# Moving the first batch's tail mixing into block 0, with the ScalarE table loaded first and some copies moved to ScalarE

## The chip, the cores and the metric

The kernel runs on one core of a Trainium2 chip. The core has five engines with queues of their own: PE (TensorE, matrix products; its weight loads are listed as PEld), DVE (VectorE), ACT (ScalarE), POOL (GpSimd) and SP (SyncE, which here issues the transfers). They work on SBUF; PE writes its results into PSUM, of which this kernel uses eight banks. The metric is the device time of one execution in microseconds (us); less is better.

## The reference

Two steps follow each other for a batch of 8, with 8 heads, 576 tokens and a head dimension of 64:

```python
kv = np.einsum('bhsd,bhse->bhde', k, v)            # linear attention, no softmax
out = np.einsum('bhsd,bhde->bhse', q, kv)
rms = np.sqrt(np.mean(out * out, axis=-1, keepdims=True) + 1e-06)
x = (out / rms * g_norm)                            # heads side by side: (8, 576, 512)
h = x.transpose(0, 2, 1) @ U @ V                    # mixes tokens, rank 32
u = x + h.transpose(0, 2, 1)
ch = np.maximum(u @ w_ch1, 0.0) @ w_ch2             # 512 -> 2048 -> 512
return u + ch
```

U, V, w_ch1 and w_ch2 arrive as float64 and are decoded to float32 on the chip from their bit patterns.

## The kernel before, in words

**Tiling.** Heads are handled in pairs (128 columns), so a batch has four pairs. The 8 x 576 = 4608 tokens are cut into nine blocks of 512 columns for the feed-forward part, so a block does not end with its batch: block 0 is the first 512 tokens of batch 0, and the last 64 tokens of batch 0 are the first columns of block 1. In a block, f runs over 16 tiles of the 2048 hidden features: `ffn1` (L365) multiplies with w1, `relu` (L372) takes the positive part, `ffn2` (L381) multiplies with w2 into four PSUM banks. Every product is made of three in a shorter format (high x high, high x low, low x high), so activations and weights are kept as a high and a low part. `relu` writes the high part on ScalarE (L377), the low part on VectorE (L378).

**Startup.** Batch 0 has no earlier block to hide behind. Its steps stand in a list `tasks` (L475 to L486), each with a place number from `PLAN` (L39); the list is sorted by that number and written out before block 0. For a pair p the steps are: `kv_step` (k transposed times v, copied into `kvb`), `out_step` (q times kv, five products, and their squares on ScalarE), `stats_step` (sums on VectorE, square root on ScalarE, reciprocal and a refinement on VectorE), `mul_step`, `xsplit_step` (high part `xh` on ScalarE, low part `xl` on VectorE), `turn_step` (transposes x by products with the identity, four 128-token tiles into one bank, `main`), `t_step` (the product with U), `t4_step` (its high and low parts into a tile `t4`), `keep_warm`, `mix_first` and `mix_rest`.

`mix_first` (L334) adds the product of `t4` and V to `main` and writes the high and low part of 512 columns of block 0's input (names `uth`, `utl`). `mix_rest` (L347) does the same for the last 64 tokens: one product with the identity (L350, listed as two instructions), one of `t4` and V (L352), a scaled copy to `ut32` (L353, by the helper at L104). `split_cols(0, p, 1)` then makes from it the high and low part of the first 64 columns of block 1 (L94 and L95). In the startup `mix_rest` stands at `PLAN["mt"]`, after all four `mix_first`; the splits of all four pairs stand in block 0.

`keep_warm` (L329) issues products whose result nobody reads, into a bank called `spare` (name `h`); its stationary operand is the pair's `t4`.

**Block 0 and later.** `prep_schedule(j + 1)` (L495) returns what is to be done beside block j, by half step: entry 2f comes after `relu` of f, entry 2f + 1 after `ffn2` of f - 1. It holds batch 1's steps during block 0. Block 0 also decodes the weights: `decode_w` for the f up to three ahead (L533 to L536). A decode is five instructions on raw bits (absolute value at L81 on ScalarE or at L83 on VectorE, then L84, L85, L87 and L89 on VectorE) and a split (L94 on ScalarE, L95 on VectorE); the first tile of each matrix is decoded in the startup, with temporaries called `early`, all others with the three buffers called `st`. The `t4` tiles of pairs 1 to 3 of batch 0 are taken from the same three buffers (L424).

**Who does what.** `ENG` (L40) names an engine for each use of the helpers `move` (L97), `minus` and `decode`: a is ScalarE, v VectorE, g GpSimd, one letter per pair or use. The helpers' own lines (L102, L104, L108, L110, L114) appear in the profile.

**Order.** The order in the program is a priority. When it is built, a scheduler that plans with estimated durations takes, for each engine, the first instruction in that order that is ready and whose tile has a free buffer; the order that it finds is fixed for each engine's queue. A tile's buffer comes free with the last instruction in the whole program that uses it.

Of the kernel before, what the change touches and what calls it, by code (L numbers as in the profile page):

```python
# [10 lines left out]
F32 = mybir.dt.float32  # L11
# [9 lines left out]
P = 128  # L21
NPAIR = H // 2
NT = 5
MAIN = 4 * P
TAIL = S - MAIN
NF = DF // P
ND = DM // P
# [9 lines left out]
STEPS0 = dict(kv=1, out=2, t=6, mix=11, gap=3)  # L37
AHEAD = dict(w1=3, w2=3)
PLAN = dict(pair=(0, 7, 13, 13), kv=(0, 0, 0, 0), out=(2, 0, 0, 6), stats=(2, 3, 3, 6), mul=(2, 3, 3, 6), xs=(11, 11, 10, 10), tr=(11, 11, 11, 14), t=(14, 14, 12, 14), t4=(18, 18, 14, 18), mix=(18, 23, 21, 23), mt=(42, 42, 42, 42), uv=6, v4=11, w0=49, w1=45, w2=38, w3=49, x0=49, warm=12, fill0=4, fill1=3, fill2=1, fill3=2, u2=60)  # L39
ENG = dict(kv='aaaaa', xh='aaaaa', xl='vvvvv', t4='avva', te='aaaa', uh='vaaa', v4='aggg', wh='ava', wl='vvv', ab='vav', u='agva')  # L40
LOADS = ['uv', 'q1', 'w10', 'kv1', 'w11', 'kv2', 'g', 'q2', 'q3', 'kv3', 'w12', 'w20', 'w13', 'w22', 'w23', 'w21', 'kv4', 'q4']
NBLK = B * S // BLK
ABS_LO = float(np.array([897 << 20], np.uint32).view(np.float32)[0])
# [4 lines left out]
def build(ctx: ExitStack, tc: tile.TileContext, kv_in, kvt0_in, kvt_in, q_in, uv_in, g_in, w1, w2, out):  # L48
    nc = tc.nc

    const = ctx.enter_context(tc.tile_pool(name="const", bufs=1))
# [11 lines left out]
    ut32 = [const.tile([P, S], F32, name=f"ut32_{c}") for c in range(ND)]  # L63
    ident = const.tile([P, P], F32, name="ident")
    g_sb = const.tile([P, 1], F32, name="g_sb")
    eps = const.tile([P, 2], F32, name="eps")
    u2 = const.tile([P, NT, 2 * R], F32R, name="u2")
    v4 = const.tile([P, S], F32R, name="v4")
    kvb = [const.tile([P, P], F32, name=f"kvb{i}") for i in range(2)]

    def weight_slot(name, shape, dtype, which, f):

        return const.tile(shape, dtype, name=name, tag=f"{which}_{f}")

    def decode(raw, tmp, n=None):
# [3 lines left out]
        bits = tmp.bitcast(U32)  # L79
        if n is None or ENG["ab"][n] == "a":  # L80
            nc.scalar.activation(out=tmp, in_=high.bitcast(F32), func=AF.Abs)  # L81
# [10 lines left out]
    def split(hi, lo, src, lo_eng):  # L92

        nc.scalar.copy(out=hi, in_=src)  # L94
        lo_eng.tensor_tensor(out=lo, in0=src, in1=hi.bitcast(F32), op=ALU.subtract)  # L95

    def move(which, n, out, in_, mul=None):  # L97

        e = ENG[which][n]
        if e == "a":  # L100
            if mul is None:
                nc.scalar.copy(out=out, in_=in_)  # L102
            else:
                nc.scalar.mul(out=out, in_=in_, mul=mul)  # L104
        else:
            eng = nc.vector if e == "v" else nc.gpsimd
            if mul is None:
                eng.tensor_copy(out=out, in_=in_)  # L108
            else:
                eng.tensor_scalar(out=out, in0=in_, scalar1=mul, scalar2=None, op0=ALU.mult)  # L110

    def minus(which, n, out, in0, in1):
        eng = nc.vector if ENG[which][n] == "v" else nc.gpsimd
        eng.tensor_tensor(out=out, in0=in0, in1=in1, op=ALU.subtract)  # L114
# [22 lines left out]
    def load_q(b, p):  # L137
        if b == 0 and 0 < p:
            qt = weight_slot(f"q0_{p}", [P, S], F32, "w1", NF - 1 - p)
        else:  # L140
            qt = ldp.tile([P, S], F32, name="q_sb")
        nc.sync.dma_start(out=qt, in_=q_in[b, p])
        loads["q", b, p] = qt
# [23 lines left out]
    def ut_of(j):  # L167
        if j not in ut:
            ut[j] = [utp.tile([P, ND, BLK], F32R, name=f"ut{s}") for s in "hl"]
        return ut[j]  # L170
# [4 lines left out]
    def bank():  # L175
        bank_no[0] += 1
        if startup[0] and bank_no[0] % (7 - NEARLY) >= 3 - NEARLY:
            return ps_y.tile([P, 512], F32, name="y")
        return ps_p.tile([P, 512], F32, name="pp")
# [28 lines left out]
    state = {}  # L208
# [103 lines left out]
    def split_cols(b, c, part, lo_eng):  # L312

        m = BLK * (b + 1) - S * b
        uh, ul = ut_of(b + part)
        if part == 0:
            src, lo = ut32[c][:, 0:m], BLK - m
        else:
            src, lo = ut32[c][:, m:S], 0
        n = src.shape[-1]  # L320
        hi, lo = uh[:, c, lo:lo + n], ul[:, c, lo:lo + n]
        if b == 0:
            split(hi, lo, src, lo_eng)
        else:
            nc.scalar.mul(out=hi, in_=src, mul=g_sb)  # L325
            nc.vector.scalar_tensor_tensor(out=lo, in0=src, scalar=g_sb, in1=hi.bitcast(F32),  # L326
                                           op0=ALU.mult, op1=ALU.subtract)

    def keep_warm(p, n):  # L329

        for _ in range(n):
            nc.tensor.matmul(spare, lhsT=state[0, p]["t4"], rhs=v4[:, 0:MAIN], start=True, stop=True)

    def mix_first(p):  # L334

        s = state[0, p]
        main = s["main"]
        for a in (0, 2):
            own = main.rearrange("p (i a j) -> p i a j", a=4, j=32)[:, :, a:a + 2]
            v = v4[:, QO[a]:QO[a] + 2 * QL[a]].rearrange("p (a t) -> p a t", a=2)[:, :, 0:P]  # L340
            nc.tensor.matmul(own, lhsT=s["t4"], rhs=v.rearrange("p a (i j) -> p i a j", j=32), start=False, stop=(a == 2))
        uh, ul = ut_of(0)
        move("uh", p, uh[:, p], main, g_sb)
        nc.vector.scalar_tensor_tensor(out=ul[:, p], in0=main, scalar=g_sb, in1=uh[:, p].bitcast(F32),
                                       op0=ALU.mult, op1=ALU.subtract)

    def mix_rest(p):  # L347
        s = state[0, p]
        tail = bank()[:, 0:TAIL]
        nc.tensor.matmul(tail, lhsT=s["x"][0:TAIL, 4, :], rhs=ident[0:TAIL, 0:TAIL], start=True, stop=False)  # L350
        v = v4[:, 0:2 * QL[0]].rearrange("p (a t) -> p a t", a=2)[:, :, P:]
        nc.tensor.matmul(tail.rearrange("p (a j) -> p a j", a=2), lhsT=s["t4"], rhs=v, start=False, stop=True)  # L352
        move("te", p, ut32[p][:, MAIN:S], tail, g_sb)  # L353
# [54 lines left out]

    load_kv(0, 0)
    load_q(0, 0)  # L410
    nc.vector.memset(kvb[0], 0.0)
    spare = ps_h.tile([P, BLK], F32, name="h")
    for _ in range(PLAN["warm"]):
        nc.tensor.matmul(spare[:, 0:P], lhsT=kvb[0], rhs=kvb[0], start=True, stop=True)
    nc.scalar.sqrt(out=kvb[0][:, 0:1], in_=kvb[0][:, 0:1])
    x0 = [x_sb] + [weight_slot(f"x{p}", [P, NT, P], F32, "w2", NF - 4 - p) for p in range(1, NPAIR)]
    xhl0 = [weight_slot(f"x{n}0", [P, nt, P], F32R, "w1", f) for n, nt, f in (("h", NT, NF - 1), ("l", 4, NF - 6))]
    for t in x0:
        nc.gpsimd.memset(t[TAIL:P, 4, :], 0.0)
    nc.gpsimd.memset(kvb[1], 0.0)  # L420
    nc.gpsimd.memset(eps[:, 0:1], 1e-6)
    nc.gpsimd.memset(eps[:, 1:2], -0.5e-6)
    make_identity(nc, ident)
    t40 = {p: st.tile([P, P], F32R, name="st") for p in (1, 2, 3)}  # L424
    early = [weight_slot(f"early{i}", [P, DM], F32, f"w{i + 1}", 9) for i in range(2)]
# [49 lines left out]
    tasks = [(PLAN["uv"], uv_step), (PLAN["v4"], v4_step), (PLAN["u2"], u2_step)]  # L475
    for p in range(NPAIR):
        for name, what in (("kv", kv_step), ("out", out_step), ("stats", stats_step), ("mul", mul_step),
                           ("xs", xsplit_step), ("tr", turn_step), ("t", t_step), ("t4", t4_step)):
            tasks.append((PLAN["pair"][p] + PLAN[name][p], lambda what=what, p=p: what(0, p)))
        tasks.append((PLAN["pair"][p] + PLAN["mix"][p], lambda p=p: keep_warm(p, PLAN[f"fill{p}"])))  # L480
        tasks.append((PLAN["pair"][p] + PLAN["mix"][p], lambda p=p: mix_first(p)))
        tasks.append((PLAN["pair"][p] + PLAN["mt"][p], lambda p=p: mix_rest(p)))
    ahead = {"w1": NEARLY, "w2": 1}
    for f in range(NEARLY):
        tasks.append((PLAN[f"w{f}"], lambda f=f: decode_w("w1", f, early[f % 2], min(f, 1))))
# [9 lines left out]
    def prep_schedule(b):  # L495

        todo = {}
        if 0 < b <= B:
            todo[1] = [lambda: [split_cols(b - 1, c, 1, nc.vector) for c in range(ND)]]
        if b < B:  # L500
            for p in range(NPAIR):
                steps = STEPS0 if b == 1 else STEPS
                base = steps["gap"] * p

                def kv(p=p):
                    kv_step(b, p)
                    nxt = (b, p + 1) if p + 1 < NPAIR else (b + 1, 0)
                    if nxt[0] < B:
                        load_kv(*nxt)

                def o(p=p):
                    for what in (out_step, stats_step, mul_step, xsplit_step, turn_step):
                        what(b, p)
                    nxt = (b, p + 1) if p + 1 < NPAIR else (b + 1, 0)
                    if nxt[0] < B:
                        load_q(*nxt)

                def t(p=p):
                    t_step(b, p)
                    t4_step(b, p)  # L520

                for at, what in (("kv", kv), ("out", o), ("t", t), ("mix", lambda p=p: mix_step(b, p))):
                    todo.setdefault(base + steps[at], []).append(what)
        return todo
# [3 lines left out]
    for j in range(NBLK):  # L528
        todo = prep_schedule(j + 1)
# [88 lines left out]
```

## Time and profile before

| | |
|---|---|
| median of 3 runs | 933.15 us (931.9 to 934.48) |
| the profiled execution's own time | 932.47 us |
| its span (first to last instruction) | 930.7 us |
| PE, DVE, ACT, POOL busy | 913.9, 430.4, 265.2, 48.1 us |
| mean granted TensorE clock | 0.994 of full |
| instructions | 12300 |

The profiled execution took 932.47 us, of which the span is 930.7. A line such as L350 is a line of the kernel before. In rows of a group, the first number behind the bar is busy time in us, the next the mean of one in ns, and behind the second bar stands the idle time of the engine just ahead of these instructions, with what ended most of it. Rows in order of time begin with the start in us and the duration. A product on float32 operands appears as two PE instructions. PE instructions overlap, so a difference of starts says more than a duration.

### The profile page before, as it was taken

To read this page: it belongs to the slowest core of one execution; us is meant where nothing else is said; L and a number is where in the kernel's file an instruction comes from. 1 tells how busy PE (TensorE), PEld (TensorE's weight loads), DVE (VectorE), ACT (ScalarE), POOL (GpSimd) and SP (SyncE) were. 2 spreads that over 40 slices of the span, in tenths; PEclk is the share of its full clock that TensorE was granted. 3 is DMA by queue.
4 is the path that set the end of the run, shared out by engine and by line. 5 is a ranking of instruction groups with operands and counts; after the bars stand their busy time and mean duration, and the time that the engine had idled before them with its cause. 6 is when DMAs were issued, how large, how long until landed. Compare 5 with 4: busy or idle time off the path is not lost.

```text
span 930.7 us, 12300 instructions
## 1 busy us (share of the span) xinstructions
PE 913.9 (98%) x4570; PEld 764.7 (82%) x4570; DVE 430.4 (46%) x945; ACT 265.2 (28%) x598; POOL 48.1 (5%) x67
## 2 busy tenths in 40 slices
PE   8899989999999999999999999999999999999998
PEld 8778867888888888888888888888788888888887
DVE  6899997444364345434344445434344331112112
ACT  5455654322232223222222223222222221111110
POOL 3000002000020002000200001000200020002000
PEclk9899999999999999999999999999999999999999
DMA  8952213221122121211121112212110010001001
GB/s 345 407 223 71 63 38 107 69 56 55 49 97 59 31 77 63 84 31 57 64 69 54 40 59 74 82 31 73 58 50 25 13 46 1 1 0 46 1 1 46
DMA packets 45036, 65.49 MB, mean 70 GB/s; under 512 B 9904, under 2 KB 28080, under 8 KB 44976
## 3 DMA queue, kind: packets, MB, share of 16 engines
q1 hardware_dynamic: 44976, 64.71, 21.2%
q8 instruction: 36, 0.59, 0.3%
q14 instruction: 24, 0.20, 0.1%
HBM read 46.97 MB, written 9.44 MB: 61 GB/s over the span
## 4 chain that ended last, share of the span: by engine, by line
PE 89%; DVE 5%; DMA 3%; SPq 1%; issue 0%; ACT 0%; POOL 0%; DVEq 0%; POOLq 0%
PE y L385 39%; PE h L368 13%; PE h L369 13%; PE h L370 13%; PE pp L195 3%; PE pp L218 2%; DMA w2raw<-w 1%; DMA g_sb<-g_in 1%; PE pp L290 1%; SPq L278 1%; PE pp L292 1%; DVE utl L326 1%; PE pp L360 1%; PE pp L220 1%; PE pp L385 1%; DVE hl L378 1%
## 5 line engine op out<-in xcount | busy, mean ns | idle before, releaser
L385 PE MATMUL y<-hh,w2s 128*128 128x512 f32 x1144 | 374.2, 394 | 2.0 <-ACT hh L377 2.0
L385 PEld LDWEIGHTS y<-hh,w2s 128*128 128x128 f32 x1144 | 207.4, 188 | 42.6 <-ACT hh L377 3.7
L378 DVE SCALAR_TENSOR_TENSOR hl<-h,hh 128x512 fp32r<-128x512 f32 x142 | 97.9, 690 | 295.7 <-ACT hh L377 294.6
L368 PE MATMUL h<-uth,w1s 128*128 128x512 f32 x568 | 224.2, 395 | 1.8 <-DVE hl L378 1.8
L385 PE MATMUL y<-hl,w2s 128*128 128x512 f32 (+1 forms) x572 | 221.2, 387 | 1.9 <-DVE hl L378 1.9
L369 PE MATMUL h<-utl,w1s 128*128 128x512 f32 x568 | 222.1, 391 | 0.0
L370 PE MATMUL h<-uth,w1s 128*128 128x512 f32 x568 | 221.6, 390 | 0.0
L377 ACT ACTIVATE hh<-h 128x512 fp32r<-128x512 f32 x142 | 84.9, 598 | 387.1 <-PE h L370 387.0
L368 PEld LDWEIGHTS h<-uth,w1s 128*128 128x128 f32 x568 | 106.7, 188 | 27.0 <-DVE hl L378 3.9
L385 PEld LDWEIGHTS y<-hl,w2s 128*128 128x128 f32 x572 | 107.4, 188 | 24.1 <-DVE hl L378 2.0
L370 PEld LDWEIGHTS h<-uth,w1s 128*128 128x128 f32 x568 | 106.7, 188 | 23.2 <-DVE w1s L95 0.3
L369 PEld LDWEIGHTS h<-utl,w1s 128*128 128x128 f32 x568 | 106.9, 188 | 21.1
L397 POOL TENSOR_TENSOR st<-st,utl 128x512 f32<-128x512 f32 x32 | 40.7, 1294 | 773.1 <-DVE st L396 770.0
L362 DVE TENSOR_TENSOR ut<-pp,ut 128x288 f32<-128x288 f32 x56 | 25.0, 456 | 51.3 <-DMA ut<-xt 40.8
L396 DVE TENSOR_TENSOR st<-y,uth 128x512 f32<-128x512 f32 x32 | 21.3, 687 | 44.5 <-PE y L385 32.7
L325 ACT ACTIVATE uth<-ut,g_sb 128x448 fp32r<-128x448 f32 (+7 forms) x56 | 27.7, 532 | 46.5 <-DVE ut L362 39.5
L234 DVE TENSOR_REDUCE sums<-x 128x10 f32<-128x640 f32 x32 | 26.2, 818 | 22.6 <-ACT x L222 22.6
L326 DVE SCALAR_TENSOR_TENSOR utl<-ut,g_sb,uth 128x448 fp32r<-128x448 f32 (+7 forms) x56 | 26.9, 513 | 11.8 <-ACT uth L325 8.0
L195 PE MATMUL pp<-kv_sb 128*128 128x128 f32 x232 | 32.3, 280 | 0.0
L195 PEld LDWEIGHTS pp<-kv_sb 128*128 128x128 f32 x232 | 30.4, 197 | 0.9
L218 PE MATMUL pp<-kvb,q_sb 128*128 128x128 f32 x224 | 30.3, 280 | 0.0
L102 ACT CAST xh<-x 128x640 fp32r<-128x640 f32 x32 | 23.2, 726 | 24.8 <-DVE x L249 24.8
(188 smaller groups left out, 682.9 us busy)
## 6 DMA issues: line engine op xcount, KB each, us to landing
kv_sb<-kv_in SPq DMA_DIRECT2D x29, 512.0 KB, 3.6
q_sb<-q_in SPq DMA_DIRECT2D x29, 288.0 KB, 2.8
w1raw<-w SPq DMA_DIRECT2D x16, 512.0 KB, 9.9
w2raw<-w SPq DMA_DIRECT2D x16, 512.0 KB, 10.1
out<-st SPq DMA_DIRECT2D x32, 256.0 KB, 2.0
ut<-xt SPq DMA_DIRECT2D x224, 20.0 KB, 1.8
ut<-xt SPq DMA_DIRECT2D x224, 16.0 KB, 1.8
kvt_sb<-kvt_in SPq DMA_DIRECT2D x27, 128.0 KB, 3.2
```

Of the source, the lines that this page charges most:

```text
L195: nc.tensor.matmul(pp[:, 0:P], lhsT=m[:, i * P:(i + 1) * P], rhs=m[:, MAIN + i * P:MAIN + (i + 1) * P], start=(i == 0 and b < NATIVE), sto ...
L218: nc.tensor.matmul(big[:, i * P:(i + 1) * P], lhsT=qt[:, TAIL + i * P:TAIL + (i + 1) * P], rhs=kb, start=True, stop=True)
L234: nc.vector.tensor_reduce(out=sums.rearrange("p (i h) -> p i h", h=2), in_=xv, axis=AX.X, op=ALU.add)
L325: nc.scalar.mul(out=hi, in_=src, mul=g_sb)
L326: nc.vector.scalar_tensor_tensor(out=lo, in0=src, scalar=g_sb, in1=hi.bitcast(F32), op0=ALU.mult, op1=ALU.subtract)
L368: nc.tensor.matmul(h, lhsT=w1s[f][0][:, d, :], rhs=uh[:, d, :], start=(d == 0), stop=False)
L369: nc.tensor.matmul(h, lhsT=w1s[f][0][:, d, :], rhs=ul[:, d, :], start=False, stop=False)
L370: nc.tensor.matmul(h, lhsT=w1s[f][1][:, d, :], rhs=uh[:, d, :], start=False, stop=(d == ND - 1))
L377: nc.scalar.activation(out=hh, in_=h, func=AF.Relu)
L378: nc.vector.scalar_tensor_tensor(out=hl, in0=h, scalar=0.0, in1=hh.bitcast(F32), op0=ALU.max, op1=ALU.subtract)
L385: nc.tensor.matmul(acc, lhsT=w2s[f][w][:, c, :], rhs=h[:, cols], start=(f == 0 and w == 0 and h is hh), stop=(f == NF - 1 and w == 1))
L397: nc.gpsimd.tensor_tensor(out=o, in0=o, in1=ul[:, c, :].bitcast(F32), op=ALU.add)
```

## The change

- `mix_rest` leaves the startup's list. In block 0's list its pair p stands at half step 1 + 2p, followed by that pair's `split_cols` (before, the four splits stood together at half step 1). Later batches keep their splits as they were.
- The products of `keep_warm` take their stationary operand from `v4` (V's parts) and not from the pair's `t4`.
- The constants `eps` get a third column; VectorE sets them first of all, and a square root on them is ScalarE's first instruction. The square root on `kvb` after the warm-up products is gone.
- `ENG`: the copies of `t4` for pairs 1 and 2, the high part of pair 0's mixed columns, and the first step of the decode for the two weight tiles of the startup are ScalarE's instead of VectorE's.

```diff
-ENG = dict(..., t4='avva', te='aaaa', uh='vaaa', ..., ab='vav', ...)
+ENG = dict(..., t4='aaaa', te='aaaa', uh='aaaa', ..., ab='aaa', ...)
...
-    eps = const.tile([P, 2], F32, name="eps")
+    eps = const.tile([P, 3], F32, name="eps")
...
-            nc.tensor.matmul(spare, lhsT=state[0, p]["t4"], rhs=v4[:, 0:MAIN], start=True, stop=True)
+            nc.tensor.matmul(spare, lhsT=v4[:, 0:P], rhs=v4[:, 0:MAIN], start=True, stop=True)
...
     load_q(0, 0)
+    nc.vector.memset(eps[:, 0:1], 1e-6)
+    nc.vector.memset(eps[:, 1:2], -0.5e-6)
+    nc.scalar.sqrt(out=eps[:, 2:3], in_=eps[:, 0:1])
     nc.vector.memset(kvb[0], 0.0)
...
-    nc.scalar.sqrt(out=kvb[0][:, 0:1], in_=kvb[0][:, 0:1])
...
-    nc.gpsimd.memset(eps[:, 0:1], 1e-6)
-    nc.gpsimd.memset(eps[:, 1:2], -0.5e-6)
...
-        tasks.append((PLAN["pair"][p] + PLAN["mt"][p], lambda p=p: mix_rest(p)))
...
         if 0 < b <= B:
-            todo[1] = [lambda: [split_cols(b - 1, c, 1, nc.vector) for c in range(ND)]]
+            if b == 1:
+                for p in range(NPAIR):
+                    todo[1 + 2 * p] = [lambda p=p: mix_rest(p), lambda p=p: split_cols(0, p, 1, nc.vector)]
+            else:
+                todo[1] = [lambda: [split_cols(b - 1, c, 1, nc.vector) for c in range(ND)]]
```

More of the change, by code (lines that the diff above doesn't have):

```diff
@@ L39 @@
 PLAN = dict(pair=(0, 7, 13, 13), kv=(0, 0, 0, 0), out=(2, 0, 0, 6), stats=(2, 3, 3, 6), mul=(2, 3, 3, 6), xs=(11, 11, 10, 10), tr=(11, 11, 11, 14), t=(14, 14, 12, 14), t4=(18, 18, 14, 18), mix=(18, 23, 21, 23), mt=(42, 42, 42, 42), uv=6, v4=11, w0=49, w1=45, w2=38, w3=49, x0=49, warm=12, fill0=4, fill1=3, fill2=1, fill3=2, u2=60)
-ENG = dict(kv='aaaaa', xh='aaaaa', xl='vvvvv', t4='avva', te='aaaa', uh='vaaa', v4='aggg', wh='ava', wl='vvv', ab='vav', u='agva')
+ENG = dict(kv='aaaaa', xh='aaaaa', xl='vvvvv', t4='aaaa', te='aaaa', uh='aaaa', v4='aggg', wh='ava', wl='vvv', ab='aaa', u='agva')
 LOADS = ['uv', 'q1', 'w10', 'kv1', 'w11', 'kv2', 'g', 'q2', 'q3', 'kv3', 'w12', 'w20', 'w13', 'w22', 'w23', 'w21', 'kv4', 'q4']
```

## The prediction, made before the changed kernel ran

> **What bounds the kernel now.** I read the page's engine line first, then a table of busy time by stage that I cut at the places where the clock and the chain of waits change, then the chain itself, then the instructions in order of time between 6 and 41 us. The page says that PE is busy throughout:
>
> ```profile
> PE 913.9 (98%) x4570; PEld 764.7 (82%) x4570; DVE 430.4 (46%) x945; ACT 265.2 (28%) x598; POOL 48.1 (5%) x67
> ```
>
> That is an average over stages with different limits, and the change touches only the first of them. Busy time by stage (columns: stretch in us, length, then busy us and instruction count of PE, PEld, DVE, ACT and POOL, the granted clock, the DMA share, GB/s):
>
> ```profile
> 6.50:9.90 3.40, 1.76 (x14) 1.45 (x13) 2.24 (x6) 2.79 (x7) 0.00 (x0) 1.00 1.02 412
> 9.90:13.30 3.40, 3.40 (x17) 3.22 (x16) 2.89 (x6) 2.18 (x9) 2.92 (x7) 0.50 0.79 305
> ...
> 24.00:36.20 12.20, 11.01 (x84) 9.43 (x84) 10.56 (x26) 4.96 (x12) 0.10 (x1) 1.00 1.04 407
> ...
> 37.20:40.60 3.40, 1.11 (x6) 0.90 (x6) 3.34 (x10) 1.78 (x7) 0.00 (x0) 1.00 1.02 407
> 40.60:47.40 6.80, 6.80 (x25) 5.95 (x26) 6.25 (x13) 4.08 (x11) 0.00 (x0) 0.50 1.03 411
> 47.40:107.10 59.70, 58.98 (x293) 48.71 (x293) 58.93 (x128) 34.23 (x71) 0.00 (x0) 1.00 0.36 128
> 107.10:153.20 46.10, 41.21 (x208) 32.67 (x206) 45.37 (x103) 25.17 (x52) 0.00 (x0) 1.00 0.20 58
> 153.20:240.00 86.80, 86.80 (x445) 73.14 (x446) 41.72 (x97) 25.58 (x62) 5.13 (x4) 1.00 0.22 64
> ```
>
> From 47.4 to 153.2 us VectorE is full: 58.93 of 59.70 and 45.37 of 46.10. In the second of these stretches PE idles 46.10 - 41.21 = 4.9 us. The chain of waits says who sets the end of that stretch:
>
> ```profile
> 150.79 0.69 DVE x L247
> 151.70 0.84 DVE xt L275
> 152.55 0.59 DVE hl L378
> 153.18 0.50 PE h L368
> ```
>
> So block 0 ends when VectorE has worked off the weight decodes, the splits and batch 1's preparation. Behind 153 us PE is full (86.80 of 86.80) and VectorE half idle; none of that work is touched, so I let it follow block 0 unchanged. **The question is therefore how much earlier VectorE gets through its queue**, and not how much PE work is saved.
>
> **The change part by part.** First, the table. These are instructions in order of time (start, duration, engine, line, operation):
>
> ```profile
> 7.39 0.49 PE L199 MATMUL pp<-kvt_sb 64*128 64x128 f32 x2
> 7.51 1.28 ACT L415 ACT_TABLE_LOAD   x1
> 8.80 0.20 ACT L415 ACTIVATE kvb<-kvb 128x1 f32<-128x1 f32 x1
> 9.04 0.43 ACT L102 COPY kvb<-pp 64x64 f32<-64x64 f32 x2
> 9.52 1.77 PE L218 MATMUL y<-kvb,q_sb 128*128 128x128 f32 x8 [1.64 <-ACT kvb L102]
> ```
>
> Pair 0's product is finished at 7.39 + 0.49 = 7.88 us, but its copy waits until 9.04 behind a second table load (1.28) and a square root (0.20) whose operand the warm-up matmuls still read. With a square root first, on a constant that VectorE has just set, there is one load, ahead of all data. The absolute values decode later under the square root's table with no further load (the L81 instructions below), so I expect no second one. Pair 0 gains up to 9.04 - 7.88 = 1.16 us. Against it stand two more one-column memsets on VectorE ahead of the one that the warm-up waits for. The trace has no such row; the 128-column memset took 0.17 us, so I bound the two between 0 and 0.34 and count 0.2. As for what arrives at the end of the stage: later pairs wait for loads of their own, so between 0 and 1.16; I take 0.5.
>
> On this load the Trainium skill, page "ScalarE: Activation LUTs", section "What ACT_TABLE_LOAD costs", gives about 1283 ns plus about 1380 ns of drain, 2.66 us for each switch. The trace agrees on the 1.28; the next activation starts 0.01 us behind it, so no such drain shows. By the page pair 0 would gain 2.66; I keep the row.
>
> Second, the moves from VectorE to ScalarE (groups: count, then busy us and mean ns of one):
>
> ```profile
> L110 DVE TENSOR_SCALAR uth<-pp,g_sb 128x512 fp32r<-128x512 f32 x1 | 0.8, 751 | 0.4 <-DMA w2raw<-w 0.4
> ...
> L83 DVE TENSOR_SCALAR early<-w2raw 128x512 uint32<-128x512 uint32 x1 | 0.4, 427 | 0.3 <-POOL early L427 0.3
> L83 DVE TENSOR_SCALAR early<-w1raw 128x512 uint32<-128x512 uint32 x1 | 0.4, 421 | 0.0
> ...
> L108 DVE CAST st<-y 64x128 fp32r<-64x128 f32 x1 | 0.3, 282 | 0.0
> L108 DVE CAST st<-pp 64x128 fp32r<-64x128 f32 x1 | 0.3, 275 | 0.0
> ```
>
> ```profile
> L81 ACT ACTIVATE st<-w1raw 128x512 f32<-128x512 f32 x5 | 3.4, 671 | 0.2 <-DVE w2s L95 0.2
> ...
> L104 ACT ACTIVATE uth<-pp,g_sb 128x512 fp32r<-128x512 f32 x2 | 1.4, 689 | 4.3 <-PE pp L341 2.6 <-PE pp L352 1.6
> ...
> L102 ACT CAST t<-pp 64x128 fp32r<-64x128 f32 x1 | 0.3, 260 | 0.1
> ```
>
> VectorE loses 0.751 + 0.427 + 0.421 + 0.282 + 0.275 = 2.16 us. ScalarE gains 0.689 + 2 x 0.671 + 2 x 0.260 = 2.55 us, and it has room: 4.96 busy of 12.2 us from 24.0 to 36.2. If that cover were gone (ScalarE busy with something else when pair 0's mixing lands), what is late is that pair's low part at L344, by at most one such instruction, 0.7 us. The whole 2.16 lies ahead of 36.2 us, where VectorE still waits for others now and then, so it counts in full only if the next work is ready. Bounds 0 and 2.16. The three on pairs 0 to 2 (1.31 together) stand in VectorE's queue ahead of pair 3's statistics; I take 1.0.
>
> Third, the last 64 tokens. Their four mixings (L350 twice, L352 once, each) leave the startup, and the unread products of `keep_warm` no longer wait for the pair they keep warm. In order of time:
>
> ```profile
> 34.08 0.43 PE L350 MATMUL y<-ident,x 64*128 64x64 f32 x2
> 34.44 0.30 PE L352 MATMUL y<-v,t 128*128 128x64 f32 x1
> ...
> 35.75 0.48 PE L369 MATMUL pp<-utl,w1s 128*128 128x512 f32 x1
> ...
> 36.65 0.40 PE L287 MATMUL y<-xl,u4w 128*64 128x128 f32 x4
> 37.31 0.26 ACT L102 CAST st<-y 64x128 fp32r<-64x128 f32 x1
> ...
> 38.01 0.35 DVE L95 TENSOR_TENSOR utl<-ut,uth 128x64 fp32r<-128x64 f32 x2
> 38.40 0.28 DVE L301 TENSOR_TENSOR st<-y,st 64x128 fp32r<-64x128 f32 x1
> ...
> 38.74 0.73 PE L332 MATMUL h<-v,st 128*128 128x512 f32 x2 [1.69 <-DVE st L301]
> 39.31 0.40 PE L341 MATMUL pp<-v,st 128*128 128x256 f32 x2
> ...
> 40.49 0.71 PE L368 MATMUL pp<-uth,w1s 128*128 128x512 f32 x1 [0.75 <-ACT uth L104]
> ```
>
> Pair 3 is the last to be mixed. Three tails sit in PE's queue between its own products (34.08 to 35.75, 1.67 us, 0.56 each), two of their splits stand ahead of its L301 on VectorE (0.35), and two unread products ahead of its mixing (38.74 to 39.31, 0.57). Taken out, block 0's last quarter of f = 0 could start 1.67 + 0.35 + 0.57 = 2.59 us before 40.49. The same PE work, 4 x 0.56 = 2.2 us, comes back in block 0, now behind f = 0 to 3. It is covered by PE's 4.9 us of idling before 153.2; without that cover it would cost 2.2. The splits (two ScalarE and one VectorE instruction per pair) run behind 36.2 us already, so VectorE's full stretch neither gains nor loses by them.
>
> What VectorE sees of the 2.59 is another matter. Its long queue starts with the decodes into the `st` buffers, and these are three, all held by the t4 of pairs 1 to 3 until the last product that reads them, which is the tail's:
>
> ```profile
> 35.03 0.30 PE L352 MATMUL y<-v,st 128*128 128x64 f32 x1
> ...
> 35.58 0.65 ACT L81 ACTIVATE st<-w1raw 128x512 f32<-128x512 f32 x1
> ...
> 36.26 0.43 DVE L84 TENSOR_SCALAR st<-st 128x512 f32<-128x512 f32 x1 [0.83 <-ACT st L81]
> ```
>
> The first decode starts 0.25 us behind the tail product that frees its buffer. In the changed program the tails stand behind f = 0's work in priority, but they need nothing later than pair 3's t4, so an order made by what is ready can still fill PE's waits with them. Bounds for VectorE: +2.59 (all of the chain's gain arrives) and -3.3 (below, the slower rival). I take 1.5, since pair 3's shorter chain is sure and the buffers' release only possibly late.
>
> **Sum:** 0.5 + 1.0 + 1.5 = 3.0 us. The profiled execution took 932.47 us (span 930.7 and 1.8 around it): 929.5. The median of the runs, 933.15, is 0.7 above that execution; the same step from it ends at 930.2. I say 929.8, between the two. What a measurement can tell from no change is about 0.3%, 2.8 us, so this stands at the edge.
>
> **Rivals.** *Hidden anyway.* VectorE and ScalarE get idle instead of early: loads and PE still pace the startup (PE 11.01 of 12.20 from 24.0 to 36.2, DMA full), the tails are again put into the same gaps and the buffers come free at the same moment. Only the table and a part of the moves count, about 1.0: 931.5. For it speaks that VectorE has slack before 36 us (10.56 of 12.20), against it that pair 3's own chain is what is cut.
>
> *The buffers are late: slower.* If the tails of pairs 1 to 3 really run in the order written, behind the rest of f = 0 and batch 1's first products, the first `st` buffer comes free not at 35.3 but about when the last one did, 39.55 plus its 0.19; the decode of w1's f = 1 then reaches VectorE 4.2 us later than 36.26. Less the 0.83 that it idles there already, 3.3 us are lost, and a full queue doesn't regain them: 935.8. It decides from the point where the buffers come more than about 2 us later than now, since the table and the moves bring 1.5. For it: the priority written; against it: PE idles just then (1.11 busy of 3.40 from 37.2).
>
> *PE sets the end and keeps its clock: more.* PE ran at half clock from 40.6 to 47.4, behind a stretch with 1.11 busy of 3.40; if free fillers and the shorter chain remove that, PE has 6.8 x 0.5 = 3.4 us more. It counts only if VectorE's queue gives way as well, so on top of the forecast at best: 926. The same happened once before, 9.9 to 13.3 at 0.50 behind 1.76 busy of 3.40.
>
> On this the Trainium skill, page "TensorE: Matmul & The Clock Gate", section "What's actually happening", has the half rate follow a window of about 3.4 us that is idle. Both windows here were partly busy, so by its wording neither drop would have come; the rows decide. By the page there would be nothing to win, and the forecast, which counts nothing for the clock, stays as it is.
>
> **How the numbers follow.** Forecast 0.45 (its own range 927.5 to 931), hidden anyway 0.27, late buffers 0.20, PE's clock too 0.08. Measured against the median, faster by over 0.3% means below 930.35: most of the forecast (0.39) and the last case (0.08) give 0.47; the rest of the forecast and nearly all of hidden anyway 0.32; late buffers and a tail of hidden anyway 0.21. The range runs from 925.5, the best case, to 935.8, the slower one.
>
> **What would show it.** Right: one table load, pair 0's L218 near 8.4; no L83, L110 or 64-row L108 on VectorE; the first L84 into `st` before 35 us; d = 3 of f = 0 at 37 to 38; VectorE's last decode and the first chain step on PE alone about 3 us earlier than 153.2, and the stretch behind it as long as before. Wrong: that L84 at 36 or later, a VectorE with more idle time before it and the same end, or tails (L352) behind f = 1 with decodes waiting for buffers.

## The result: 2.2% slower

The changed kernel took 953.73 us in the median of four runs (953.6 to 955.36), the kernel before 933.34 beside it (931.9 to 934.48). The ratio is 1.0222 with a 95% interval of 1.0207 to 1.0237: about 20 us slower, outside the predicted range of 925.5 to 935.8. The profiled execution took 953.6 us, with a span of 951.8 where the one of before had 930.7. Of all executions below, one of e11 took 1847.9 us, in a slow state, and its times are given without that one.

**What the 21.1 us of span are.** The engine line of the changed kernel's page:

```profile
PE 917.5 (96%) x4570; PEld 767.0 (81%) x4570; DVE 430.1 (45%) x942; ACT 267.9 (28%) x602; POOL 48.4 (5%) x65
```

PE has the same 4570 instructions. It is busy for 917.5 us instead of 913.9, which is 3.6 more, and idle for 951.8 - 917.5 = 34.3 us instead of 930.7 - 913.9 = 16.8, which is 17.5 more. Together that is 21.1: PE waits, and a part of its work runs longer.

**Where it waits.** Busy time by stage of the changed kernel (stretch, length, then busy us and instruction count of PE, PEld, DVE, ACT, POOL, granted clock, DMA share, GB/s):

```profile
36.20:47.40 11.20, 5.96 (x26) 4.22 (x26) 7.30 (x17) 5.77 (x14) 0.00 (x0) 0.76 1.03 409
47.40:69.40 22.00, 12.07 (x53) 9.70 (x51) 16.18 (x31) 8.20 (x17) 0.00 (x0) 0.74 0.60 221
69.40:92.00 22.60, 14.95 (x61) 12.21 (x60) 22.10 (x53) 13.92 (x35) 0.22 (x1) 0.62 0.29 89
92.00:165.00 73.00, 72.13 (x361) 59.75 (x360) 72.03 (x157) 41.38 (x83) 0.00 (x0) 1.00 0.17 49
```

The same stretches of the kernel before, from 36.2 us on:

```profile
36.20:47.40 11.20, 8.76 (x42) 7.46 (x41) 10.52 (x24) 6.86 (x20) 0.00 (x0) 0.70 1.02 408
47.40:69.40 22.00, 21.62 (x96) 17.57 (x95) 21.69 (x48) 11.87 (x22) 0.00 (x0) 1.00 0.57 219
69.40:92.00 22.60, 22.29 (x121) 18.88 (x122) 22.14 (x48) 13.04 (x29) 0.00 (x0) 1.00 0.23 73
92.00:165.00 73.00, 68.08 (x345) 54.92 (x344) 67.31 (x150) 38.54 (x83) 5.13 (x4) 1.00 0.23 71
```

From 36.2 to 92 us PE is busy for 5.96 + 12.07 + 14.95 = 32.98 us where it had 8.76 + 21.62 + 22.29 = 52.67: 19.7 us of busy time are missing, and PE ran 140 instructions instead of 259. From 47.4 to 69.4 us VectorE, which was full there, idles too (16.18 of 22.00): no engine sets the pace in this stretch, only waits do. From 69.4 on VectorE is full again (22.10 of 22.60), but PE still waits. From 92 to 165 us PE is busier than before (72.13 against 68.08) and so gets some 4 us back.

**What is waited for: the decodes.** Instructions of the changed kernel in order of time (start, duration, engine, line; idle time before in brackets), between 40 and 61 us:

```profile
40.84 0.43 PE L350 MATMUL pp<-ident,x 64*128 64x64 f32 x2 [1.19 <-DVE hl L378]
41.21 0.30 PE L352 MATMUL pp<-v,st 128*128 128x64 f32 x1
42.23 0.43 DVE L84 TENSOR_SCALAR st<-st 128x512 f32<-128x512 f32 x1 [0.72 <-ACT st L81]
...
56.22 0.66 ACT L81 ACTIVATE st<-w2raw 128x512 f32<-128x512 f32 x1 [0.76 <-DVE w1s L95]
56.91 0.43 DVE L84 TENSOR_SCALAR st<-st 128x512 f32<-128x512 f32 x1 [0.73 <-ACT st L81]
58.32 0.30 PE L352 MATMUL pp<-v,st 128*128 128x64 f32 x1
...
59.34 0.62 ACT L94 CAST w2s<-st 128x512 fp32r<-128x512 f32 x1 [2.46 <-DVE st L89]
59.99 0.69 DVE L95 TENSOR_TENSOR w2s<-st,w2s 128x512 fp32r<-128x512 f32 x1 [0.74 <-ACT w2s L94]
60.72 0.66 ACT L81 ACTIVATE st<-w2raw 128x512 f32<-128x512 f32 x1 [0.76 <-DVE w2s L95]
```

The first decode into an `st` buffer reaches VectorE at 42.23 us, right behind the tail product at 41.21 that frees the buffer; before, it was at 36.26. The other tails that read `st` run as late as 58.32 and 72.2, so until then two of the three buffers, or one, stay held. One decode begins when the last has ended: the absolute values (L81) start at 41.54, 46.32, 51.72, 56.22, 60.72 and 65.21, that is 4.5 to 5.4 us apart. In the round that is shown VectorE waits 0.73 for L81 and 0.74 for L94.

**And a second wait.** Further on in the same order of time:

```profile
71.83 0.43 PE L350 MATMUL pp<-ident,x 64*128 64x64 f32 x2 [2.25 <-DVE ts L305]
72.20 0.30 PE L352 MATMUL pp<-v,st 128*128 128x64 f32 x1
72.39 0.22 POOL L427 MEMSET early<- 128x1 f32 x1 [55.55 <-PE pp L350]
73.69 0.66 ACT L81 ACTIVATE early<-w2raw 128x512 f32<-128x512 f32 x1
...
84.41 0.80 PE L385 MATMUL y<-hh,w2s 128*128 128x512 f32 x1 [1.52 <-ACT w2s L102]
```

The rows of the same memset and the same product in the kernel before:

```profile
33.22 0.10 POOL L427 MEMSET early<- 128x1 f32 x1 [17.07 <-DVE xh L263]
...
49.82 1.07 PE L385 MATMUL y<-hh,w2s 128*128 128x512 f32 x4
```

POOL's one-column memset at L427 claims the second `early` buffer, in which the first tile of w2 is decoded. That buffer lies in the same place in SBUF as pair 3's x. In the kernel before, POOL waited 17.1 us for that place, and its release came from pair 3's L263; here it waits 55.55, for pair 3's tail (L350). So w2's tile 0 is decoded from 73.69, and `ffn2` begins at 84.41 instead of 49.82. `h` has one bank, and `hh` and `hl` have two buffers each, so `ffn1` can't run ahead for long meanwhile.

What the prediction forecast of the startup itself did come, in order of time of the changed kernel (its L414 is L411 of the kernel before):

```profile
0.89 0.17 DVE L414 MEMSET kvb<- 128x128 f32 x1
...
7.71 0.41 ACT L102 COPY kvb<-pp 64x64 f32<-64x64 f32 x2
8.17 1.16 PE L218 MATMUL y<-kvb,q_sb 128*128 128x128 f32 x8 [1.23 <-ACT kvb L102]
...
21.15 2.49 PE L332 MATMUL h<-v 128*128 128x512 f32 x10
23.48 1.05 PE L272 MATMUL pp<-ident,x 128*128 128x128 f32 x8
24.37 1.06 PE L218 MATMUL y<-kvb,q 128*128 128x128 f32 x8
...
38.12 0.48 PE L368 MATMUL pp<-uth,w1s 128*128 128x512 f32 x1
```

Pair 0's copy starts at 7.71 instead of 9.04, and the last quarter of f = 0 at 38.12 instead of 40.49. What is new here is the ten unread products in one piece, 2.49 us from 21.15, ahead of a turn (L272) and a query product (L218, before at 23.60).

### The profile page after: what moved, and what is told of

Its sections match the earlier page's. It is cut to its first block, busy times and chain, and to the rows that moved or that the text cites. A ratio compares the mean times of both kernels' runs of the same rounds, so it can differ in the third digit from the quotient of the medians.

```text
span 951.8 us, 12297 instructions
## 1 busy us (share of the span) xinstructions
PE 917.5 (96%) x4570; PEld 767.0 (81%) x4570; DVE 430.1 (45%) x942; ACT 267.9 (28%) x602; POOL 48.4 (5%) x65
## 4 chain that ended last, share of the span: by engine, by line
PE 85%; DMA 7%; DVE 6%; SPq 1%; issue 0%; POOL 0%; ACT 0%; DVEq 0%; POOLq 0%; ACTq 0%
PE y L385 38%; PE h L368 13%; PE h L369 13%; PE h L370 13%; DMA w2raw<-w 3%; PE pp L195 2%; PE pp L218 2%; DMA q_sb<-q_in 1%; DVE st L87 1%; DMA w1raw<-w 1%; PE pp L290 1%; DMA kv<-kv_in 1%; DVE st L89 1%; PE pp L360 1%; PE pp L292 1%; PE pp L385 1%
## 5 line engine op out<-in xcount | busy, mean ns | idle before, releaser
L378 DVE SCALAR_TENSOR_TENSOR hl<-h,hh 128x512 fp32r<-128x512 f32 x142 | 97.9, 689 | 311.2 <-ACT hh L377 310.1
L218 PE MATMUL pp<-kvb,q_sb 128*128 128x128 f32 x224 | 31.6, 287 | 8.2 <-ACT kvb L102 8.1
L218 PEld LDWEIGHTS pp<-kvb,q_sb 128*128 128x128 f32 x224 | 29.7, 201 | 9.4 <-ACT kvb L102 8.8
## 6 DMA issues: line engine op xcount, KB each, us to landing
w1raw<-w SPq DMA_DIRECT2D x16, 512.0 KB, 10.2
```

Source lines behind the costliest of these rows:

```text
L218: nc.tensor.matmul(big[:, i * P:(i + 1) * P], lhsT=qt[:, TAIL + i * P:TAIL + (i + 1) * P], rhs=kb, start=True, stop=True)
L378: nc.vector.scalar_tensor_tensor(out=hl, in0=h, scalar=0.0, in1=hh.bitcast(F32), op0=ALU.max, op1=ALU.subtract)
```

## The experiments

The theory after the result: the tails run late, and until then they hold two things, the `st` buffers (hold 1) and the place of pair 3's x (hold 2). Rivals: it is another part of the change; one hold alone is enough of a cause; or it is the lateness itself and not what is held.

### Which part of the change

**e1.** The kernel before with only the tails moved:

```diff
-        tasks.append((PLAN["pair"][p] + PLAN["mt"][p], lambda p=p: mix_rest(p)))
...
+            if b == 1:
+                for p in range(NPAIR):
+                    todo[1 + 2 * p] = [lambda p=p: mix_rest(p), lambda p=p: split_cols(0, p, 1, nc.vector)]
```

> The kernel before with nothing but the tails moved into block 0. If the move alone makes the loss (both theories below): 952 to 956 us, with the first product of ffn2 near 84 us again and three late tails. If the loss needs the other three edits as well (free fillers that shift the order, ScalarE's longer queue): within 5 us of 933.

Measured: 955.58 us, ratio 1.0241 (1.0226 to 1.0255). The tails that read `st` run at 40.86, 57.90 and 72.19 us and the first `ffn2` at 85.00, much as in the changed kernel. The move alone makes the whole loss.

**e2.** The changed kernel with the tails back in the startup (table, ScalarE's copies and the unread products on V stay; the expectations call the unread products fillers):

```diff
+        tasks.append((PLAN["pair"][p] + PLAN["mt"][p], lambda p=p: mix_rest(p)))
...
-            if b == 1:
-                for p in range(NPAIR):
-                    todo[1 + 2 * p] = ...
```

> The changed kernel with the tails back in the startup: table first, moves to ScalarE and free fillers alone. By the prediction's own sum these bring 0.5 + 1.0 and 0.57 from the fillers, about 2 us: 931.3 against 933.3. By the rival of the prediction that gives these gains back as idle time: 933 within 0.5.

Measured: 934.84 us, 1.0015 (1.0006 to 1.0023). Both expectations missed: the rest gains nothing and even costs some 0.6 to 2.1 us, by the interval. Its unread products again run in one piece, and the first decode into `st` comes at 36.27, as before.

### Which of the two holds

**e3.** Hold 1 removed from the changed kernel: the `t4` of pairs 1 to 3 get places of their own (those of w1's tiles 12 to 14, which are loaded late); their memsets move behind the first loads.

```diff
-    t40 = {p: st.tile([P, P], F32R, name="st") for p in (1, 2, 3)}
+    t40 = {p: weight_slot(f"t40_{p}", [P, P], F32R, "w1", NF - 5 + p) for p in (1, 2, 3)}
```

> The changed kernel with the t4 of pairs 1 to 3 in slots of w1's tiles 12 to 14 instead of the three decode buffers, so that no tail holds a decode buffer. Theory A (decodes in a single buffer from 42 to 66 us make the loss): decodes overlap from 36 us on, the end falls to 933 to 937. Theory B (the decode of w2's tile 0 waits for pair 3's x, so that no ffn2 can start): first ffn2 still behind the last tail, near 80 us, and the end at 945 to 952.

Measured: 954.5 us, 1.0227 (1.0213 to 1.0241): no gain. Two rows of its busy time by stage:

```profile
47.40:69.40 22.00, 16.57 (x84) 12.81 (x83) 21.94 (x50) 14.57 (x34) 0.00 (x0) 0.77 0.63 220
69.40:92.00 22.60, 15.60 (x65) 12.71 (x65) 18.70 (x46) 11.54 (x28) 0.10 (x1) 0.62 0.48 154
```

In order of time, the first `ffn2`:

```profile
83.20 0.77 PE L385 MATMUL y<-hh,w2s 128*128 128x512 f32 x1
```

VectorE is full now (21.94 of 22.00), so the decodes overlap; but `ffn2` still starts at 83.20, and PE idles for 5.4 us of 22.0 and 7.0 of 22.6. Hold 2 alone costs as much as both, a little more than the 952 us that either theory expected at most.

**e4.** Hold 2 removed instead: one `early` buffer for both tiles of the startup.

```diff
-    early = [weight_slot(f"early{i}", [P, DM], F32, f"w{i + 1}", 9) for i in range(2)]
+    early = [weight_slot("early0", [P, DM], F32, "w1", 9)]
```

> The changed kernel with one buffer for both decodes of the startup, so that the decode of w2's tile 0 no longer waits for the slot of pair 3's x; the decode buffers stay held by t4. Theory B: first ffn2 before 50 us and the end at 933 to 938. Theory A: the decodes still go one after another until 66 us, first ffn2 earlier but block 0 short of weights, 943 to 952.

Measured: 954.26 us (950.65 to 959.28), 1.0229 (1.0193 to 1.0265): again no gain. Busy time of the middle stage:

```profile
47.40:69.40 22.00, 13.35 (x44) 10.06 (x45) 14.57 (x26) 6.88 (x14) 0.00 (x0) 0.77 0.45 168
```

In order of time, the first `ffn2`:

```profile
43.40 0.96 PE L385 MATMUL y<-hh,w2s 128*128 128x512 f32 x3 [0.47 <-ACT hh L377]
```

`ffn2` starts at 43.40, earlier than in the kernel before, but VectorE idles (14.57 of 22.00): the decodes go one at a time. Hold 1 alone also costs as much as both. The tails ran at 36.99, 46.70, 69.81 and 79.47 us, and the first decode into `st` reached VectorE at 47.73, later than in the changed kernel.

**e5.** Both removed:

```diff
+    t40 = {p: weight_slot(f"t40_{p}", ...) for p in (1, 2, 3)}
+    early = [weight_slot("early0", [P, DM], F32, "w1", 9)]
```

> The changed kernel with both holds gone at once: t4 in slots of w1's tiles 12 to 14, one buffer for both decodes of the startup. Theory C (two holds of the same price lie side by side, each alone costs the 20 us): 933 to 938, first ffn2 before 50 us and decodes overlapping from 36 us. If a third cause remains behind them (the tails wait for one of three banks and are late themselves): 945 or more.

Measured: 933.84 us, 1.0005 (0.9995 to 1.0016): the loss is gone. The tail products as one line's instructions (durations in ns: least, middle and most; then first and last start):

```profile
L352 PE MATMUL pp<-v,t x4: 297/297/297, 45.9 to 79.8; 128*128 128x64 f32 x4
```

Busy time of the two stages:

```profile
47.40:69.40 22.00, 20.21 (x101) 15.73 (x99) 21.73 (x47) 13.24 (x29) 0.00 (x0) 1.00 0.59 210
69.40:92.00 22.60, 22.60 (x121) 18.63 (x120) 21.70 (x49) 12.82 (x30) 0.00 (x0) 1.00 0.47 151
```

The tails are as late as in the changed kernel, 45.9 to 79.8 us, and PE and VectorE are full again. The first `ffn2` starts at 54.83 and not before 50 as expected. So the lateness itself costs nothing. The four kernels form a square: both holds 953.73, either one 954.5 and 954.26, none 933.84. The two waits lie side by side and each is long enough, so removing one shows nothing. The order was planned anew for each of them, and the last tail ran at 75.47 us in e3 and 79.47 in e4, where the changed kernel has 72.2: that either hold is enough is shown, but not its exact price in the changed kernel.

### Why the tails are late

**e6.** In the startup `bank()` also gives out the four banks called `y`, and three tails of the kernel before write into those (L350 at 34.08 and L352 at 35.03 in the prediction's rows do). Once block 0 has begun it gives out `pp` alone: the tails that were moved and batch 1's first steps take their banks from the same three. Here the tails of the changed kernel write into the bank of the unread products instead:

```diff
-        tail = bank()[:, 0:TAIL]
+        tail = spare[:, p * TAIL:(p + 1) * TAIL]
```

> The changed kernel, but the four tails write into the bank of the unread products instead of taking one of the three others. Block 0's f = 1 needs that bank, so the order is forced: all tails ahead of f = 1. Theory C in its full form (late tails are the cause, through whatever they hold): last L352 before 45 us, first ffn2 near 50 us, the end at 930 to 937. If the tails' lateness is not the cause: 945 or more.

Measured: 934.12 us, 1.0014 (1.0004 to 1.0024). The tails that read `st`, in the same view:

```profile
L352 PE MATMUL h<-v,st x3: 193/194/297, 30.0 to 38.8; 128*128 128x64 f32 x3
```

In that bank they run at 30.0 to 38.8 us from the same place in the program, and the loss is gone without either hold being touched. So PE had time for them. The edit also forces their order, since the `h` of f = 1 needs this bank after them. That it is the wait for a bank that makes them late fits two rows of the changed kernel: one L350 (40.84) starts right behind the L378 that reads f = 0's `pp` bank, another (71.83) right behind the L305 that reads one. The tail between them (L350 at 57.91) shows no wait of its own; it stands in PE's queue behind the `ffn1` of f = 2 and a product of batch 1.

### What the smaller parts are worth

**e7.** The kernel before with the table first and ScalarE's copies; tails and unread products as before:

```diff
-ENG = dict(..., t4='avva', te='aaaa', uh='vaaa', ..., ab='vav', ...)
+ENG = dict(..., t4='aaaa', te='aaaa', uh='aaaa', ..., ab='aaa', ...)
...
+    nc.scalar.sqrt(out=eps[:, 2:3], in_=eps[:, 0:1])
     nc.vector.memset(kvb[0], 0.0)
...
-    nc.scalar.sqrt(out=kvb[0][:, 0:1], in_=kvb[0][:, 0:1])
```

> The kernel before with only the early table and the moves to ScalarE; tails in the startup, fillers reading t4 as before. If the ten free fillers, which ran as one piece of 2.35 us ahead of pair 3's q product, ate what the other edits gained: faster than the three edits together (934.8) by 1 to 3 us, so 931.8 to 933.8. If the decode's start is held by the tails' buffers in any case: 934 to 935, the same as with free fillers.

Measured: 931.77 us, 0.9989 (0.998 to 0.9999): a gain of about 1 us, and the interval nearly reaches 1. In order of time:

```profile
33.24 0.42 DVE L84 TENSOR_SCALAR st<-st 128x512 f32<-128x512 f32 x1
...
37.20 0.51 PE L368 MATMUL pp<-uth,w1s 128*128 128x512 f32 x1 [0.94 <-ACT uth L104]
```

Busy time by stage from 36.2:

```profile
36.20:47.40 11.20, 10.26 (x54) 8.30 (x53) 11.20 (x25) 7.83 (x19) 0.00 (x0) 1.00 1.03 410
47.40:69.40 22.00, 18.96 (x84) 14.19 (x82) 21.95 (x49) 10.69 (x18) 0.00 (x0) 1.00 0.57 217
```

The first decode is 3.0 us earlier than in the kernel before (36.26), f = 0's last quarter 3.3 (40.49), and the half clock from 40.6 us is gone (1.00 against 0.70). Then PE waits for VectorE's full queue from 47 us on (18.96 of 22.00, before 21.62), and about 1 of the 3 us is left at the end.

**e11 and e12.** Each of the two edits of that diff alone: the table first (e11),

> The kernel before with the early table alone. Prediction's term: 0.5, so 932.5. If the table alone keeps the clock from falling at 10 us (pair 0's copy no longer 1.16 us late) and pair 1 gains with it: 931 to 932.

932.92 us in the median of eleven runs, 0.9996 (0.9985 to 1.0006); and ScalarE's copies (e12, the line `ENG`),

> The kernel before with the five instructions moved to ScalarE and nothing else. Prediction's term: 1.0, so 932.0. If VectorE only idles instead: 933 within 0.6. The sum of this run's and the early table's differences, against 1.2 for both together, shows whether the two gains are one and the same.

932.33 us, 0.9996 (0.9986 to 1.0006), with the first decode at 33.19. Neither can be told from zero alone. The early start of the decodes is there with the copies alone.

### The unread products

**e8.** e6 with the unread products waiting for `t4`, as before:

```diff
-            nc.tensor.matmul(spare, lhsT=v4[:, 0:P], ...
+            nc.tensor.matmul(spare, lhsT=state[0, p]["t4"], ...
```

> As the run with the tails in the unread products' bank, with fillers reading t4 as before. If the piece of ten fillers costs its 2.35 us of PE at the point where pair 3 is next: 1 to 2.5 us below that run. If pair 3 has that slack: within 0.7 us of it.

Measured: 940.33 us, 1.0075 (1.0059 to 1.0091): the expectation missed, in sign too. In order of time, its last unread products, its tails and its first decode:

```profile
36.01 0.70 PE L332 MATMUL h<-v,st 128*128 128x512 f32 x2
...
37.24 0.30 PE L352 MATMUL h<-v,t 128*128 128x64 f32 x1
...
38.51 0.30 PE L352 MATMUL h<-v,st 128*128 128x64 f32 x1
...
39.55 0.43 DVE L84 TENSOR_SCALAR st<-st 128x512 f32<-128x512 f32 x1 [0.96 <-ACT st L81]
...
41.74 0.30 PE L352 MATMUL h<-v,st 128*128 128x64 f32 x1
```

Now the two kinds of product share one bank, and the tails stand behind all unread products of the program: even pair 0's tail, ready long before, runs only after pair 3's unread products at 36.01. The first decode starts at 39.55, 3.3 us later than in the kernel before, and this kernel is some 7 us slower than that one. That the shared bank sets this order fits the trace and was not tried by itself. The run mixes two things, and says nothing of the unread products alone.

**e9.** The same edit on e5, where the two don't share a bank:

> The run with both holds gone (933.84), with fillers reading t4 as before. If the free fillers cost 2 to 3 us wherever they stand: 930.5 to 932. If what they cost depends on the order found around them (the two runs with the tails in the fillers' bank went the other way, 934.1 against 940.3): 933 to 937.

Measured: 931.39 us, 0.9979 (0.997 to 0.9987), 2.4 below e5's. In e5 the unread products on V, ready from the start, run between 21.49 and 24.4 us, and a query product (L218) starts at 25.74; with `t4` they are spread from 25.96 to 50.4, and it starts at 23.62. So those on V cost some 2.4 us more than those on `t4`.

**e10.** And none at all (the first twelve, the warm-up, stay; the products left out belong to no result), with the table, ScalarE's copies and the tails in the startup:

```diff
-PLAN = dict(..., fill0=4, fill1=3, fill2=1, fill3=2, ...)
+PLAN = dict(..., fill0=0, fill1=0, fill2=0, fill3=0, ...)
```

> Early table, moves to ScalarE, tails in the startup, and no unread products at all after the first twelve (they belong to no result). If the fillers' PE time is what separated 934.8 (free fillers) from 931.8 (fillers that wait for t4): 931 to 932.5. If fillers earn their time by keeping PE's clock up: a stretch at half clock before 48 us and 933 to 936.

Measured: 929.25 us (928.95 to 931.46), 0.9964 (0.995 to 0.9978): faster than both kernels, and below both of its expectations. Busy time by stage:

```profile
0.70:36.20 35.50, 28.96 (x221) 25.83 (x221) 25.80 (x66) 20.34 (x57) 7.37 (x29) 1.00 0.97 373
36.20:47.40 11.20, 10.39 (x53) 8.49 (x54) 11.20 (x25) 7.89 (x19) 0.00 (x0) 1.00 1.03 409
```

In order of time:

```profile
20.94 1.10 PE L272 MATMUL pp<-ident,x 128*128 128x128 f32 x8
21.88 1.06 PE L218 MATMUL y<-kvb,q 128*128 128x128 f32 x8
```

Against e2, which differs by these ten products alone, that is some 5 us (934.84 - 929.25 = 5.6 by the medians, 1.0015 - 0.9964 = 0.51%, 4.8 us, by the ratios). In e2 this turn starts at 23.47 and this L218 at 24.36, some 2.5 us later, and the granted clock is 0.70 from 36.2 to 47.4 us where it is 1.00 here; how the rest of the 5 us comes about is not shown. Against e7, which has the same ten products on `t4`, it is 2.3 us (0.9989 - 0.9964 = 0.25%). So in this startup they cost time in either form.

## Why the prediction was wrong, by its own steps

- **What bounds block 0: right as far as it went.** VectorE's queue set the end of the stage, and the kernels here whose first decode starts later than before (the changed one, e1, e4 and e8, by 3.3 to 11.5 us) all lose. e3 starts it early and loses too, by the other hold. But what sets VectorE's queue is when buffers come free, and the change moved that.
- **The tails, third term: this is the step that failed.** The prediction said that the tails "need nothing later than pair 3's t4, so an order made by what is ready can still fill PE's waits with them". They need one thing more, a PSUM bank. In block 0 only the three `pp` banks are given out, and f = 0's product and batch 1's steps use these too. With another bank the tails did run early (e6: 30.0 to 38.8 us); with the three they ran at up to 72.2. So the term came out at some -20 us and not +1.5: to 65 us the decodes went one at a time, and until the last tail had run w2's first tile could not be decoded. Whether PE's 4.9 us of idling covers the tails' 2.2 us of work was never the question.
- **The chain of pair 3 did get shorter.** Forecast 2.59 us, measured 40.49 - 38.12 = 2.37 us for f = 0's last quarter. None of it counted.
- **The rival "the buffers are late: slower" had the mechanism, not the size.** It priced one late first decode at 3.3 us (it came 42.23 - 36.26 = 6.0 us late) and then let the decodes go on three buffers. In truth two of the three stayed held until 58.3 us and one until 72.2, and to 65 us each decode began 4.5 to 5.4 us behind the last. Its argument against itself, that PE idles just then, doesn't bear on a wait for a bank. By e4 this hold alone is enough for some 20 us. It would have had to be priced to the last tail and not to the first.
- **The second hold was not in the prediction at all.** `mix_rest` is also the last reader of x, whose place the decode of w2's first tile needs. The row in which POOL's L427 waits 17.1 us for pair 3's L263 stood in the trace before. By e3 this hold alone is enough for some 20 us too.
- **The table, first term: mechanism right, but L218's time is in part luck.** One load, ahead of all data, and L218 at 8.17 (8.4 forecast). Pair 0's copy came 1.33 us earlier, more than the 1.16 forecast as the most; but its product also ended at 6.46 + 0.48 = 6.94 us and not at 7.88, since in this execution the warm-up products took 4.52 us (5.49 before). The copy then still waited 0.77, behind the absolute values of U and V (L81). With 5.49 us of warm-up in both, L218 starts at 8.76 with the table first (e7) and at 8.95 without (e12). The two memsets cost 0.06, from 0.83 to 0.89, and not 0.2. At the end, 0.5 was forecast and e11 can't be told from zero.
- **The moves, second term: in size.** 1.0 was forecast; e12's interval holds zero and reaches to 1.3 us (0.9986), table and moves together brought about 1 (e7). The bounds held.
- **The unread products: wrong sign.** Counted as a gain of 0.57 in pair 3's chain and otherwise free; on V they cost 2.4 us against the old form (e9 to e5), and 2.4 to 3.1 in e2 against e7 (by the ratios and by the medians), and the old form costs 2.3 us against none (e7 to e10). In the trace they run ahead of a turn and a query product.
- **The clock.** The forecast counted nothing for it. In the changed kernel the low clock lasted longer: 0.76, 0.74 and 0.62 in the three stages to 92 us, where the kernel before had 0.70, 1.00 and 1.00, and PE is busy for 3.6 us longer over the span.
- **Two sums don't come out of the prediction's own rows.** A first buffer that comes free at 39.55 + 0.19 = 39.74 instead of 35.03 + 0.30 = 35.33 us is 4.4 us late, and not 4.2. And the low end of the range, 925.5, lies below the best case that it is taken from (929.8 - 3.4 = 926.4, or its 926). Neither matters for what failed.

## What to carry to other kernels

When a step is moved later, list every tile for which it is the last reader, and for each what next takes that place: the move delays all of these to the last of the moved steps, not to the first. Ask also which pool its results come from, since a step that only waits for a bank is as late as those that get the banks first. And when two waits lie side by side, removing one shows nothing; remove both before either is called innocent.

## What was not expected of the hardware

In one stretch of the changed kernel work with gaps did not bring the granted clock back from half. Its busy time, cut every 3.4 us:

```profile
74.60:78.00 3.40, 2.88 (x13) 2.37 (x12) 3.40 (x12) 2.09 (x7) 0.00 (x0) 0.50 0.30 101
78.00:81.40 3.40, 1.76 (x9) 1.47 (x8) 3.40 (x6) 1.09 (x2) 0.00 (x0) 0.50 0.30 87
81.40:84.80 3.40, 1.50 (x9) 1.32 (x10) 3.34 (x7) 2.69 (x6) 0.00 (x0) 0.50 0.26 83
84.80:88.20 3.40, 3.40 (x10) 2.63 (x9) 3.40 (x9) 2.03 (x5) 0.00 (x0) 0.50 0.13 30
88.20:91.60 3.40, 3.40 (x16) 2.84 (x16) 3.02 (x9) 1.07 (x4) 0.00 (x0) 0.77 0.53 174
```

The clock stays at 0.50 through 10.2 us with 2.88, 1.76 and 1.50 of 3.4 us busy and through one stretch that is full, and comes back in the next (0.77): PE works without a gap from 84.41 on. The Trainium skill, page "TensorE: Matmul & The Clock Gate", section "What's actually happening", has the full rate come back after about 3.4 us of sustained activity; these rows agree with that. In this stretch a gap thus cost PE twice, as idle time and as half clock in the work behind it. How idle a stretch must be for the clock to fall isn't settled by these runs.

And the unread products of the startup weren't needed for the clock: without them (e10) it was 1.00 in each of the five stages to 165 us, of which two stand above. The kernel before, with them, had 0.70 from 36.2 to 47.4 and 0.50 from 9.9 to 13.3 (in the prediction's rows). They aren't what made it fall there either: e7, which has them in the same form, had 1.00 in all five in its profiled execution.
